# The seven-product output stage of a two-layer feed-forward kernel: order of the low parts, and which engine does sums and copies

## The chip, the cores and the metric

The kernel runs on one core of a Trainium2 chip. A core has TensorE (PE, matrix products; its weight loads are listed as PEld), VectorE (DVE), ScalarE (ACT), GpSimd (POOL) and SyncE (SP, which issues the DMAs). Each engine works through its own queue in the order in which the kernel wrote the instructions; an instruction waits for the semaphores of what it reads, and all that stands behind it on that engine waits too. The metric is the device time of one execution in microseconds (us).

## The reference

Causal attention with a decay (4 batches, 8 heads, 576 tokens, 64 wide) gives 2304 token rows of 512. Two feed-forward layers follow, each 512 to 2048 to 512:

```
x = x @ w_in;  g = h * clip(h + 3, 0, 6) / 6;  x = g @ w_out          (layer 1)
h = x @ w_in2; g = max(h, 0) + alpha * min(h, 0);  out = g @ w_out2   (layer 2)
```

All is float32. A float32 matrix product is done as three products of parts: each operand is split into a high part (rounded by ACT, `nc.scalar.copy` into a float32r tile) and a low part (operand minus high part), and high x high, high x low and low x high are added.

## The kernel before

**Tiling.** Token rows are taken in three blocks of 768 (`p` = 0, 1, 2), the 2048 hidden features in eight groups of 256 (`g`). One pair is a set `(ff, g, p)`; layer 2 ends with the eight sets of block `p` = 2, in the order `g` = 6, 7, 0, 1, 2, 3, 4, 5. A set makes the hidden values of 256 features for 768 tokens by seven block products (Strassen's scheme in the form of Winograd, 2 x 2 blocks of features and model width against two halves of tokens); each is `product`, six matmuls of 128x384. While PE does the products of one set, it does between them the output pieces of the set before, so each group of matmuls has work of another kind around it.

**The seven sets.** For the first seven of the last eight sets (`seven`), the output product too is done in seven block products (`piece7`). The hidden values are blocks of features x tokens: `gt["f", n, i]`, token half `n`, feature tile `i`. In the code's names a11 = (0,0), a12 = (0,1), a21 = (1,0), a22 = (1,1). Out of these come four sums on GpSimd (`sums`, L762): 5 = a22 + a21, 6 = (5) - a11, 7 = a11 - a21, 3 = a12 - (6). The seven operands 4 (a22), 5, 1 (a11), 6, 7, 2 (a12), 3 each get a high part by ACT (`high7`, L757) and a low part by GpSimd (`low7`, L760). The weights have four sums of their own, made early and stored in DRAM; for each set they are fetched, and split in two halves `h` by `weights7` (high L952 on ACT, low L955 on VectorE). The four plain blocks of the hidden values end with the slope, the second half of the activation (L740 on VectorE), after a first half on ACT (L731).

**Order of the work.** The kernel writes it out by hand. `now` counts steps; each character of a sequence is a step, a digit a product, `q` the next piece of the set before. In this stage the sequence is `SEQ7 = "1q5qq6qq3qq7qq2q4q"` with the pieces `PLAN7 = 4, 5, 45, 1, 6, 16, 7, 7-, 2, 3, 23`. A piece of one number is that block product for two row tiles of the half (six matmuls of 128x256), one of two numbers the third row tile of two block products, `7-` that of one. `later(d, fn)` puts instructions d steps on, in the order in which they were registered for that step; `aside` puts them behind these. So the low part of operand 6, for instance, is written seven steps after product 2 and that of 2 three steps after product 4, and GpSimd's queue in a set is: 5, low of 4, low of 5, 6, 7, low of 1, 3, low of 2, low of 6, low of 7, low of 3. In a piece's three matmuls for one tile the low part of the hidden values is read by the third.

**Where the products are summed.** A piece ends in a PSUM tile `o` (three buffers in turn: a piece can't start until the one three before it has been read out). For the first of the seven sets `flush` copies it to its place in SBUF (`kept`), for the others VectorE adds it (L922). After the seventh set, while the last set `(1, 5, 2)` runs, the seven kept products are summed into the four output blocks (`sum7`, L930): 6 = 1 + 6, 7 = 6 + 7, 6 = 6 + 5, 4 = 7 - 4, 5 = 7 + 5, 2 = 1 + 2, 3 = 6 + 3, each as one instruction of 128x512 and one of 128x256. The last set then has six plain pieces (`piece`, L842, six matmuls of 128x512), first three of token half 1, then three of half 0; each is added by VectorE to a summed block (L860) and stored.

Of the kernel before, what the change touches and what calls it, by code (L numbers as in the profile page):

```python
# [8 lines left out]
F32 = mybir.dt.float32  # L9
# [5 lines left out]
ALU = mybir.AluOpType  # L15
# [6 lines left out]
def decay_attention_ffn2_kernel(ctx, tc, qk, v, f, wi1, wo1, wi2, wo2, alpha, out):  # L22
    nc = tc.nc
# [685 lines left out]
    def later(d, fn):  # L709
        at.setdefault(now[0] + d, []).append(fn)  # L710

    def aside(d, fn):
        behind.setdefault(now[0] + int(d), []).append(fn)

    def activate(s, gt, i, n, h, d):
        ff, g, p = s
        if n not in gt and s not in seven:
            gt[n] = {}
        hold = {}

        def first():
            if s in seven:
                t = P["tp"].tile([128, NB], F32, tag="t", name="t") if (n, i) != (0, 1) else temp("wa")[:, 0:NB]
                gt["f", n, i] = t
            else:
                t = P["tp"].tile([128, NB], F32, tag="t", name="t")
            if ff == 0:
                nc.scalar.activation(out=t, in_=h(), func=AF.Relu, bias=three, scale=1.0)
                hold["g"] = t
                return  # L730
            nc.scalar.activation(out=t, in_=h(), func=AF.Relu, scale=-1.0)  # L731
            hold["g"] = t

        def second():
            g32 = hold["g"]
            if ff == 0:
                nc.vector.scalar_tensor_tensor(out=g32, in0=g32, scalar=6.0, in1=h(), op0=ALU.min, op1=ALU.mult)  # L737
            else:
                m = g * FT + i
                nc.vector.scalar_tensor_tensor(out=g32, in0=g32, scalar=alpha_sb[:, m:m + 1], in1=h(),  # L740
                                               op0=ALU.mult, op1=ALU.add)

        def third():
            gt[n][i] = P["gp"].tile([128, 2, NB], F32R, tag=f"g{n}", name=f"g{n}", bufs=3 - n)
            nc.scalar.copy(out=gt[n][i][:, 0], in_=hold["g"])  # L745
            nc.gpsimd.tensor_sub(out=gt[n][i][:, 1], in0=hold["g"], in1=gt[n][i][:, 0].bitcast(F32))  # L746

        def high7(k, t):
            if k in (2, 3):
                j = gorder[ff][1].index(g)  # L750
                o = XS[0][0].rearrange("p a b c -> p (a b c)").rearrange("p (k n) -> p k n", k=7)[:, 2 * (j % 2) + k - 2]
                o = o.rearrange("p (a n) -> p a n", a=2)
            else:
                tag = "g1" if k in (4, 5) else "g0"
                o = P["gp"].tile([128, 2, NB], F32R, tag=tag, name=tag, bufs=2 if k in (4, 5) else 3)
            gt[k] = o
            nc.scalar.copy(out=o[:, 0], in_=t)  # L757

        def low7(k, t):
            nc.gpsimd.tensor_sub(out=gt[k][:, 1], in0=t, in1=gt[k][:, 0].bitcast(F32))  # L760

        def sums():  # L762
            a11, a12, a21, a22 = (gt.get(("f", x, y)) for x in range(2) for y in range(2))
            if (n, i) == (1, 1):
                gt["f", 5] = temp("wc")[:, 0:NB]
                nc.gpsimd.tensor_add(out=gt["f", 5], in0=a22, in1=a21)
            elif (n, i) == (0, 0):
                gt["f", 6], gt["f", 7] = temp("wd")[:, 0:NB], a21
                nc.gpsimd.tensor_sub(out=gt["f", 6], in0=gt["f", 5], in1=a11)
                nc.gpsimd.tensor_sub(out=a21, in0=a11, in1=a21)  # L770
            else:
                gt["f", 3] = temp("wc")[:, 0:NB]
                nc.gpsimd.tensor_sub(out=gt["f", 3], in0=a12, in1=gt["f", 6])

        later(d, first)
        later(d + 1, second)
        if s in seven:
            k = {(1, 1): 4, (0, 0): 1, (0, 1): 2}.get((n, i))
            if k:
                more = {4: (5,), 1: (6, 7), 2: (3,)}[k]  # L780
                gap = len(more)
                later(d + 2, lambda: high7(k, hold["g"]))
                later(d + 2, sums)
                later(d + 3, lambda: low7(k, hold["g"]))
                for x in more:
                    later(d + 3 + gap, lambda x=x: high7(x, gt["f", x]))
                    later(d + 4 + gap, lambda x=x: low7(x, gt["f", x]))
            return
        later(d + 1, third)

# [77 lines left out]
    def temp(tag):  # L868
        return wtmp.tile([128, KH, 256], F32, tag=tag, name=tag).rearrange("p k n -> p (k n)")
# [16 lines left out]
    def tees(j):  # L886
        t = XS[0][1].rearrange("p a b c -> p (a b c)")[:, 4 * DM * (j % 2):4 * DM * (j % 2) + 4 * DM]
        return t.rearrange("p (a k n) -> p a k n", a=2, k=4)

    def piece7(s, gt, text):  # L890
        ff, g, p = s
        j = gorder[ff][1].index(g)
        wo, tw, kept, hd = wt[ff, g, 1], tees(j), keep7(), DM // 2
        plain = {1: (0, 0), 2: (1, 0), 3: (1, 1)}
        o = P["ps_o"].tile([128, 512], F32, tag="o", name="o")
        work = [(int(text[0]), c) for c in range(2)] if len(text) == 1 else [(int(k), 2) for k in text if k != "-"]
        for slot, (k, c) in enumerate(work):
            a = gt[k]
            if k in plain:
                t, x = plain[k]  # L900
                b = [wo[:, e, t, hd * x:hd * x + hd] for e in range(2)]
            else:
                b = [tw[:, e, WT7[k]] for e in range(2)]
            cs = slice(c * 128, c * 128 + 128)
            for e, (x, y) in enumerate(((a[:, 0], b[0]), (a[:, 0], b[1]), (a[:, 1], b[0]))):
                nc.tensor.matmul(out=o[:, hd * slot:hd * slot + hd], lhsT=x[:, cs], rhs=y,  # L906
                                 start=slot == 0 and e == 0, stop=e == 2, skip_group_check=slot > 0)
        src = o.rearrange("p (a n) -> p a n", a=2)
        if len(text) == 1:
            dst = kept[int(text)][0]  # L910
        elif text[1] != "-":
            dst = kept[text]
        else:
            dst, src = kept[int(text[0])][1], o[:, 0:hd]

        def flush():
            if j == 0 and len(text) == 1:
                nc.scalar.copy(out=dst, in_=src)
            elif j == 0:
                nc.vector.tensor_copy(out=dst, in_=src)  # L920
            else:
                nc.vector.tensor_add(out=dst, in0=src, in1=dst)  # L922

        later(0, flush)
        if s != seven[-1]:
            return

        def sum7(wait, engine, d, x, y, op):
            for part in range(2):
                later(wait, lambda part=part: engine.tensor_tensor(out=kept[d][part], in0=kept[x][part],  # L930
                                                                   in1=kept[y][part], op=op))

        if text == "16":
            sum7(1, nc.gpsimd, 6, 1, 6, ALU.add)
        if text == "7-":
            sum7(1, nc.gpsimd, 7, 6, 7, ALU.add)
            sum7(3, nc.gpsimd, 6, 6, 5, ALU.add)
            sum7(4, nc.vector, 4, 7, 4, ALU.subtract)
            sum7(5, nc.vector, 5, 7, 5, ALU.add)
        if text == "23":  # L940
            sum7(2, nc.vector, 2, 1, 2, ALU.add)
            sum7(3, nc.vector, 3, 6, 3, ALU.add)

    def weights7(s):
        ff, g, p = s
        tw = tees(gorder[ff][1].index(g))

        def fetch7():
            nc.sync.dma_start(out=tw[:, 1].bitcast(F32), in_=wt_d[g])

        def high7(h):
            nc.scalar.copy(out=tw[:, 0, 2 * h:2 * h + 2], in_=tw[:, 1, 2 * h:2 * h + 2].bitcast(F32))  # L952

        def low7(h):
            nc.vector.tensor_sub(out=tw[:, 1, 2 * h:2 * h + 2], in0=tw[:, 1, 2 * h:2 * h + 2].bitcast(F32),  # L955
                                 in1=tw[:, 0, 2 * h:2 * h + 2].bitcast(F32))

        if s == seven[0]:
            ops = conv_ops(1, 0, tags="cdabc")
            for t, names in ((0, "p2 p3"), (4, "v1 v3"), (5, "v2 u0"), (6, "v4 u1")):  # L960
                for name in names.split():
                    aside(t, ops[name])
        fetch7()
        for h in range(2):
            aside(8 + 2 * h, lambda h=h: high7(h))
            aside(9 + 2 * h, lambda h=h: low7(h))
# [156 lines left out]
```

## Time and profile before

| | us |
|---|---|
| median of 3 runs (lowest, highest) | 967.99 (966.4, 969.34) |
| the profiled execution, its own time | 969.33 |
| its span, first to last instruction | 967.5 |
| busy: PE, PEld, DVE, POOL, ACT | 948.3, 866.5, 733.1, 665.4, 550.3 |

The span is what lies between the first and the last instruction of the profiled execution; the rest of that execution's own time, 1.83 us, lies around it. Busy times are over the whole span. The seven sets and the last set take the stretch from 834 us of the span to its end; the rows below are times in us from the span's start.

### The profile page before, as it was taken

To read this page: it belongs to the slowest core of one execution; us is meant where nothing else is said; L and a number is where in the kernel's file an instruction comes from. 1 tells how busy PE (TensorE), PEld (TensorE's weight loads), DVE (VectorE), ACT (ScalarE), POOL (GpSimd) and SP (SyncE) were. 2 spreads that over 40 slices of the span, in tenths; PEclk is the share of its full clock that TensorE was granted. 3 is DMA by queue.
4 is the path that set the end of the run, shared out by engine and by line. 5 is a ranking of instruction groups with operands and counts; after the bars stand their busy time and mean duration, and the time that the engine had idled before them with its cause. 6 is when DMAs were issued, how large, how long until landed. Compare 5 with 4: busy or idle time off the path is not lost.

```text
span 967.5 us, 16523 instructions
## 1 busy us (share of the span) xinstructions
PE 948.3 (98%) x5714; PEld 866.5 (90%) x5714; DVE 733.1 (76%) x1291; ACT 550.3 (57%) x1352; POOL 665.4 (69%) x661
## 2 busy tenths in 40 slices
PE   8999999999999999999999999999999999999997
PEld 5777777789999999999999999898989999899995
DVE  7899999767787887777788573378778877576866
ACT  5888888856655555554654456545545455454441
POOL 7678998656666556684773497667675779457574
PEclk9999999999999999999999999999999999999998
DMA  6766777202354244111778540415553411646431
GB/s 212 228 202 187 227 240 226 85 23 71 137 186 185 90 172 178 63 45 42 290 255 325 205 166 34 176 62 188 196 207 103 177 37 65 251 165 260 169 159 66
DMA packets 39512, 153.71 MB, mean 159 GB/s; under 512 B 5228, under 2 KB 5228, under 8 KB 36324
## 3 DMA queue, kind: packets, MB, share of 16 engines
q1 hardware_dynamic: 39424, 152.65, 44.9%
q8 instruction: 45, 0.74, 0.3%
q14 instruction: 39, 0.32, 0.1%
q10 hardware_dynamic: 4, 0.00, 0.0%
HBM read 101.40 MB, written 47.09 MB: 153 GB/s over the span
## 4 chain that ended last, share of the span: by engine, by line
PE 83%; DVE 7%; POOL 5%; issue 3%; ACT 2%; DMA 1%; DVEq 0%; POOLq 0%; ACTq 0%; SPq 0%
PE o L840 19%; PE hA L802 18%; PE o L842 15%; PE hC L802 9%; PE hB L802 4%; PE pv L492 4%; PE tp L434 4%; PE sc L403 2%; PE sc L404 2%; PE o L906 2%; POOL g L760 1%; PE sc L415 1%; PE sc L417 1%; PE sc L405 1%; PE tr L472 1%
## 5 line engine op out<-in xcount | busy, mean ns | idle before, releaser
L746 POOL TENSOR_TENSOR g<-t,g 128x384 fp32r<-128x384 f32 x164 | 177.5, 1083 | 173.9 <-ACT g L745 167.2
L840 PE MATMUL o<-g,wo 128*128 128x384 f32 x1152 | 230.9, 339 | 1.2 <-POOL g L746 1.1
L802 PE MATMUL hA<-xh,wi 128*128 128x384 f32 x768 | 225.2, 337 | 0.6 <-ACT p L386 0.3
L840 PEld LDWEIGHTS o<-g,wo 128*128 128x128 f32 x1152 | 204.1, 188 | 2.4 <-POOL g L746 2.0
L745 ACT CAST g<-t 128x384 fp32r<-128x384 f32 x164 | 84.3, 514 | 149.4 <-DVE t L737 74.7
L842 PE MATMUL o<-wo,g 128*128 128x512 f32 x612 | 160.7, 399 | 3.4 <-DVE r L922 3.4
L802 PEld LDWEIGHTS hA<-xh,wi 128*128 128x128 f32 x768 | 141.6, 188 | 3.3 <-DVE hD L816 0.6
L842 PEld LDWEIGHTS o<-wo,g 128*128 128x128 f32 x612 | 115.6, 191 | 22.7 <-DVE r L922 3.8
L802 PE MATMUL hA<-xl,wi 128*128 128x384 f32 x384 | 129.5, 337 | 0.0
L849 DVE SCALAR_TENSOR_TENSOR r<-o,r 128x384 f32<-128x384 f32 x168 | 92.1, 551 | 47.2 <-PE o L840 46.3
L802 PE MATMUL hC<-xh,wi 128*128 128x384 f32 x384 | 114.1, 338 | 0.0
L860 DVE TENSOR_TENSOR r<-o,r 128x512 f32<-128x512 f32 x90 | 61.7, 686 | 43.2 <-PE o L842 42.9
L386 ACT ACTIVATE p<-sc,nm 128x128 f32<-128x128 f32 (+2 forms) x144 | 80.1, 561 | 19.4 <-DVE nm L379 16.4
L379 DVE TENSOR_REDUCE nm<-sc 128x1 f32<-128x128 f32 (+2 forms) x144 | 71.2, 506 | 11.7 <-PE sc L405 6.4
L802 PEld LDWEIGHTS hA<-xl,wi 128*128 128x128 f32 x384 | 72.2, 188 | 2.2
L802 PEld LDWEIGHTS hC<-xh,wi 128*128 128x128 f32 x384 | 70.9, 188 | 1.5 <-issue 0.2
L264 POOL TENSOR_TENSOR xl<-r,xh 128x384 fp32r<-128x384 f32 x59 | 68.5, 1173 | 2.1 <-ACT xh L259 1.6
L434 PE MATMUL tp<-ident,p 128*128 128x128 f32 x384 | 66.8, 277 | 0.3 <-ACT pt L449 0.3
L802 PE MATMUL hC<-xl,wi 128*128 128x384 f32 x192 | 64.8, 337 | 0.0
L807 ACT COPY s<-hA 128x384 f32<-128x384 f32 x96 | 45.8, 477 | 25.9 <-PE hA L802 25.6
L802 PE MATMUL hB<-xh,wi 128*128 128x384 f32 x192 | 57.1, 338 | 0.0
L816 DVE TENSOR_TENSOR hC<-hC,s 128x384 f32<-128x384 f32 x48 | 27.0, 563 | 37.1 <-PE hC L802 31.5
(203 smaller groups left out, 2073.3 us busy)
## 6 DMA issues: line engine op xcount, KB each, us to landing
wid<-wi SPq DMA_DIRECT2D x24, 896.0 KB
wi<-wid SPq DMA_DIRECT2D x12, 1792.0 KB
rqk<-in_qk SPq DMA_DIRECT2D x32, 608.0 KB
raw<-in_wi SPq DMA_DIRECT2D x32, 512.0 KB
raw<-in_wo SPq DMA_DIRECT2D x32, 512.0 KB
wod<-wo SPq DMA_DIRECT2D x24, 512.0 KB
wo<-wod SPq DMA_DIRECT2D x12, 1024.0 KB
vt<-in_v SPq DMA_DIRECT2D x16, 320.0 KB
```

Of the source, the lines that this page charges most:

```text
L264: e.tensor_sub(out=XS[k][1][:, b, c], in0=x, in1=XS[k][0][:, b, c].bitcast(F32))
L379: last = waits("V", nc.vector.tensor_reduce(out=nm, in_=src, axis=AX.X if n == 1 else AX.XY, op=ALU.max, negate=True), last)
L386: last = waits("A", nc.scalar.activation(out=o, in_=src, func=AF.Exp, bias=nm, scale=1.0, accum_out=dst), last)
L434: nc.tensor.transpose(tp[:, j, :], pt[:, 128 * j:128 * j + 128], ident)
L745: nc.scalar.copy(out=gt[n][i][:, 0], in_=hold["g"])
L746: nc.gpsimd.tensor_sub(out=gt[n][i][:, 1], in0=hold["g"], in1=gt[n][i][:, 0].bitcast(F32))
L802: nc.tensor.matmul(out=h, lhsT=a, rhs=b[:, x, kc], start=new and kc + e == 0, stop=kc == KH - 1 and e == 2, skip_group_check=not new)
L807: nc.scalar.copy(out=c[k], in_=h)
L840: nc.tensor.matmul(out=o[:, 0:NB], lhsT=a[:, cs], rhs=b, start=st, stop=sp)
L842: nc.tensor.matmul(out=o, lhsT=b[:, cs], rhs=a, start=st, stop=sp)
L849: later(0, lambda: nc.vector.scalar_tensor_tensor(out=acc, in0=o[:, 0:NB], scalar=1.0 / 6.0, in1=acc, op0=ALU.mult, op1=ALU.add))
L860: nc.vector.tensor_add(out=acc, in0=o, in1=acc)
```

## The change

Five edits, all in the stage of the seven sets:

- operand 6 is made by VectorE instead of GpSimd;
- the high and low parts of 6 are written two steps earlier, those of 7 one step earlier; 5 and 3 stay. GpSimd's queue in a set becomes: 5, low of 4, low of 5, 7, low of 1, 3, low of 6, low of 2, low of 7, low of 3;
- the first set's copies out of PSUM: pieces 4 and 5 go from ACT to VectorE, 16 and 23 from VectorE to ACT;
- of the last sums, 4 and 5 are written one step after piece 23 (they were at the two steps ahead of and with it), so behind the last set's slopes and behind the read-out of 23, and 2 goes from VectorE to GpSimd;
- the low parts of the weight sums go from VectorE to GpSimd.

```diff
             elif (n, i) == (0, 0):
                 gt["f", 6], gt["f", 7] = temp("wd")[:, 0:NB], a21
-                nc.gpsimd.tensor_sub(out=gt["f", 6], in0=gt["f", 5], in1=a11)
+                nc.vector.tensor_sub(out=gt["f", 6], in0=gt["f", 5], in1=a11)
                 nc.gpsimd.tensor_sub(out=a21, in0=a11, in1=a21)
...
             if k:
-                more = {4: (5,), 1: (6, 7), 2: (3,)}[k]
-                gap = len(more)
                 later(d + 2, lambda: high7(k, hold["g"]))
                 later(d + 2, sums)
                 later(d + 3, lambda: low7(k, hold["g"]))
-                for x in more:
-                    later(d + 3 + gap, lambda x=x: high7(x, gt["f", x]))
-                    later(d + 4 + gap, lambda x=x: low7(x, gt["f", x]))
+                for x, e in {4: ((5, 4),), 1: ((6, 3), (7, 4)), 2: ((3, 4),)}[k]:
+                    later(d + e, lambda x=x: high7(x, gt["f", x]))
+                    later(d + e + 1, lambda x=x: low7(x, gt["f", x]))
...
-            if j == 0 and len(text) == 1:
+            if j == 0 and text in "16723":
                 nc.scalar.copy(out=dst, in_=src)
...
             sum7(3, nc.gpsimd, 6, 6, 5, ALU.add)
-            sum7(4, nc.vector, 4, 7, 4, ALU.subtract)
-            sum7(5, nc.vector, 5, 7, 5, ALU.add)
         if text == "23":
-            sum7(2, nc.vector, 2, 1, 2, ALU.add)
+            sum7(1, nc.vector, 4, 7, 4, ALU.subtract)
+            sum7(1, nc.vector, 5, 7, 5, ALU.add)
+            sum7(2, nc.gpsimd, 2, 1, 2, ALU.add)
             sum7(3, nc.vector, 3, 6, 3, ALU.add)
...
         def low7(h):
-            nc.vector.tensor_sub(out=tw[:, 1, 2 * h:2 * h + 2], in0=tw[:, 1, 2 * h:2 * h + 2].bitcast(F32),
+            nc.gpsimd.tensor_sub(out=tw[:, 1, 2 * h:2 * h + 2], in0=tw[:, 1, 2 * h:2 * h + 2].bitcast(F32),
                                  in1=tw[:, 0, 2 * h:2 * h + 2].bitcast(F32))
```

## Rows read from the trace of the kernel before

**Rows 1.** Page, part 4: the chain that ended last, by engine.
```profile
PE 83%; DVE 7%; POOL 5%; issue 3%; ACT 2%; DMA 1%; DVEq 0%; POOLq 0%; ACTq 0%; SPq 0%
```
**Rows 2.** Waits, 834 to 967.5: who waited for whom: total us, times, longest.
```profile
POOL wc L766 <- DVE t L740: 36.3, 6, 10.7
...
PE o L906 <- POOL g L760: 6.3, 8, 1.4
...
PE o L842 <- DVE r L922: 3.4, 1, 3.4
```
**Rows 3.** Windows, one set: length, busy of PE, PEld, DVE, ACT, POOL, clock, DMA.
```profile
867.50:883.40 15.90, 15.08 (x107) 14.87 (x106) 11.84 (x21) 7.30 (x16) 10.79 (x11) 1.00 0.56 199
```
**Rows 4.** Timeline of PE: start, us, line, tiles, [idle before]; first set, third set.
```profile
841.60 1.45 PE L906 MATMUL o<-xl,g 128*128 128x256 f32 x10 [1.44 <-POOL g L760]
...
876.81 0.74 PE L906 MATMUL o<-xl,g 128*128 128x256 f32 x4 [0.82 <-POOL g L760]
```
**Rows 5.** Timeline of POOL, one set: 6, low of 2, low of 6, next 5.
```profile
870.88 1.01 POOL L769 TENSOR_TENSOR wd<-wc,t 128x384 f32<-128x384 f32 x1
...
874.78 1.02 POOL L760 TENSOR_TENSOR xh<-wa,xh 128x384 fp32r<-128x384 f32 x1
875.76 1.00 POOL L760 TENSOR_TENSOR g<-wd,g 128x384 fp32r<-128x384 f32 x1
...
883.83 1.01 POOL L766 TENSOR_TENSOR wc<-t 128x384 f32<-128x384 f32 x1 [5.12 <-DVE t L740]
```
**Rows 6.** Timeline of DVE in that set: the slope of block a12.
```profile
870.26 0.61 DVE L740 SCALAR_TENSOR_TENSOR wa<-wa,alpha_sb,hA 128x384 f32<-128x384 f32 x1 [0.18 <-ACT wa L731]
```
**Rows 7.** Timeline of POOL in the first set: operand 6.
```profile
838.61 1.02 POOL L769 TENSOR_TENSOR wd<-wc,t 128x384 f32<-128x384 f32 x1 [1.20 <-issue]
```
**Rows 8.** Lines L264, L955, L930: count, ns lowest/median/highest, first and last start.
```profile
L264 DVE TENSOR_TENSOR xl<-r,xh x25: 541/728/1640, 212.8 to 819.4; 128x384 fp32r<-128x384 f32 x25
...
L955 DVE TENSOR_TENSOR xl<-xl x14: 678/681/1375, 834.1 to 929.9; 128x512 fp32r<-128x512 f32 x14
...
L930 POOL TENSOR_TENSOR raw<-raw x2: 1287/1294/1300, 945.8 to 948.7; 128x512 f32<-128x512 f32 x2
```
**Rows 9.** Timeline of DVE at the end: sums 4 and 5, slopes, flush of 23.
```profile
950.03 2.63 DVE L930 TENSOR_TENSOR r<-raw,r 128x512 f32<-128x512 f32 x2 [1.76 <-POOL raw L930]
...
951.16 1.50 DVE L930 TENSOR_TENSOR r<-raw,r 128x256 f32<-128x256 f32 x1
952.58 0.60 DVE L740 SCALAR_TENSOR_TENSOR t<-t,alpha_sb,hB 128x384 f32<-128x384 f32 x1
...
953.71 0.41 DVE L930 TENSOR_TENSOR r<-raw,r 128x256 f32<-128x256 f32 x1
954.20 0.61 DVE L740 SCALAR_TENSOR_TENSOR t<-t,alpha_sb,hA 128x384 f32<-128x384 f32 x1
954.74 0.68 DVE L922 TENSOR_TENSOR r<-o,r 128x512 f32<-128x512 f32 x1
```
**Rows 10.** Timeline of POOL at the end: 6 = 6 + 5, first part.
```profile
950.64 1.73 POOL L930 TENSOR_TENSOR raw<-raw,r 128x512 f32<-128x512 f32 x1
```
**Rows 11.** Timeline of PE at the end: the last six pieces.
```profile
949.16 2.94 PE L842 MATMUL o<-wo,g 128*128 128x512 f32 x12
955.47 8.46 PE L842 MATMUL o<-wo,g 128*128 128x512 f32 x24 [3.38 <-DVE r L922]
```
**Rows 12.** Windows at the end; the last but two figures: the granted clock, as share.
```profile
954.00:955.00 1.00, 0.00 (x0) 0.00 (x0) 0.92 (x3) 0.32 (x2) 0.98 (x1) 0.70 0.00 0
...
961.00:962.00 1.00, 1.00 (x5) 0.77 (x5) 0.69 (x1) 0.00 (x0) 0.00 (x0) 0.89 0.03 8
```
**Rows 13.** Timeline of DVE: the last instruction on it.
```profile
963.97 0.69 DVE L860 TENSOR_TENSOR r<-o,r 128x512 f32<-128x512 f32 x1 [0.71 <-PE o L842]
```

## The prediction

> **What bounds the kernel now.** The chain of waits comes first [rows 1]: PE has 83% of it, so the end moves only where PE is idle or slowed. The list of waits over the last stretch, which all five edits touch, shows what PE waits for there [rows 2]: the low parts made by POOL (6.3 us in eight waits, all ahead of output pieces) and one read-out of a PSUM buffer by DVE (3.4 us). The windows show that one set lasts 15.90 us, of which PE is busy 15.08 [rows 3]: the 0.82 missing is one wait in each set. The PE timeline shows it: in the third set PE stands at 875.99 with piece 6 begun and goes on at 876.81, when POOL has ended the low part of 6 (875.76 + 1.00) [rows 4, 5]. The first set has a larger one: PE waits 1.44 us for the low part of 5, until 841.60 [rows 4]. POOL isn't short of time: it is busy 10.79 of 15.90 and idle 5.12 in one piece before operand 5 of the next set [rows 3, 5]. It does the right work in the wrong order.
>
> The second loss is at the end. PE stops 3.38 us before the fourth-to-last piece, because the buffer it needs holds piece 23, whose read-out (954.74, 0.68) stands in DVE's queue behind sum 4, a slope, sum 5 and the other slope [rows 9, 11]. The idle PE also loses its clock: 0.70 on the mean over 954 to 955 (so 1.0 down to 0.5 at about 954.4), back at about 961.2 [rows 12]. These are the two levels 2.4 and 1.2 GHz. Twelve matmuls took 2.94 us before the stop, 24 took 8.46 after it where twice 2.94 is 5.88 [rows 11], so the half clock costs about 2.6 us.
>
> **Order of the low parts and the sum on VectorE.** The instructions per set stay the same in number; POOL loses operand 6 (1.01) and the low part of 6 moves ahead of that of 2. POOL's queue from 870.88 on, where it had operand 6, is now 7, low of 1, 3, low of 6, at 0.97 from start to start (874.78 to 875.76 is 0.98): low of 6 runs 873.8 to 874.8, and PE asks for it at 875.99 [rows 4, 5]. That is 1.2 us of slack where 0.8 was missing. What is late next? Low of 2 then ends by 875.8 and low of 7 by 876.8, both for pieces that come after piece 6, so nothing is.
>
> Operand 6 on DVE has no row. The nearest is a subtraction of the same size with both inputs in SBUF: 0.54 alone, 0.73 at the median, 1.64 at most [rows 8]. It goes in ahead of the slope of a12, which is queued behind it and had started at 870.26 after 0.18 idle [rows 6]: 6 from 870.1 to 870.6 or 871.7, the slope then done between 871.2 and 872.3. Who waits for these: 3 on POOL, which isn't up before 872.8, and ACT's high part of 6, which low of 6 needs at 873.8. Both ends of the range cost nothing; I take 0.73 to 1.0. DVE's read-outs behind it shift by as much, within its idle time (11.84 busy of 15.90 [rows 3]).
>
> **Weight lows on POOL.** Two per set leave DVE (0.68 each, up to 1.38) and come to POOL at about 1.29 each, the price of a 128x512 subtraction there [rows 8]. They are written behind POOL's chain of the set, into the 5.12 idle before the next operand 5: 2.6 of 5.1, so they are covered. If that cover were gone they would delay operand 5 and eat the 1.2 of slack first. On DVE the two slots ahead of the slope that releases operand 5 become free, so POOL's chain starts up to 0.7 earlier: the slack grows.
>
> In the first set it is tighter. Low of 5 ended at 841.6; POOL had waited 1.20 there before operand 6 [rows 7]. Without that gap (-1.20), without 6 (-0.97), with the slope some 0.6 earlier, and with a weight low now between operand 5 and low of 4 (+1.29), it ends at about 840.1, and PE needs it at 841.60 - 1.44 = 840.16 [rows 4]. No wait, or a few tenths. The first set's copies swap between ACT and DVE, both with idle time around them: nothing.
>
> Sum of this stage: 6.3 [rows 2] less 0.4 left in the first set: **5.9 us**. Bounds: 3.5, if half of the waits of sets two to seven come back through POOL instructions slowed beside DVE, to 6.3.
>
> **The end.** DVE is idle for 1.76 until 950.03 [rows 9], so free at 948.3; before, sum 4 stood in front and waited for POOL. Now the first slope runs 948.3 to 948.9, the second starts 1.0 after its end as in the rows (953.18 to 954.20, ACT's work for it lies between), so 949.9 to 950.5, and piece 23 is read out by 951.2 instead of 955.4. PE needs this at 952.1: the 3.38 wait goes, and the third piece ends at 953.5.
>
> But the next piece needs the buffer of the first one, and its read-out is now queued behind sums 4 and 5 on DVE. Each is a 512 and a 256 instruction. Alone they cost 0.68 + 0.41 [rows 8, 9]; beside POOL's sums the pair took 2.63, in it a 256 that took 1.50 [rows 9]. So the read-out starts between 951.2 + 2.2 = 953.4 and 951.2 + 5.3 = 956.5. POOL has 6 + 5, two low parts and sum 2 in its queue without a gap from 950.64 on, so the row beside POOL is the nearest: I take 956.0, read out at 956.7. PE stops from 953.5 to 956.7, 3.2 us, nearly as long as before, one piece later.
>
> A rule of the Trainium skill bears on this choice ("SBUF — State Buffer", section "SBUF: two separate sides"): VectorE instructions with two SBUF inputs and GpSimd instructions that read SBUF share a port pair, and whoever starts first holds it for the whole instruction while the other is blocked. The 1.50 instruction agrees: it ended 0.29 after POOL's (950.64 + 1.73 = 952.37) [rows 9, 10]. By that rule the four parts of sums 4 and 5 each wait out one POOL instruction and the read-out starts at about 956.1; with no such lock, at 953.4.
>
> A stop of 3.2 us looks like the one that lost the clock, so I expect the fall again: 18 matmuls at 0.245 are 4.4, plus about 2.7 for the half clock, so PE ends at 963.8 against 963.9. Without the fall it ends at 961.1. With sums at their lowest price it ends near 958.6; at their highest, with all 18 at half clock, near 966. I take a gain of **0.2 us**, bounds -2.0 and 5.3. Sum 2 on POOL ends by 958.5, before its block is read. After the last add (963.97 [rows 13]) nothing changes.
>
> **Sum.** 5.9 + 0.2 = 6.1 off the profiled execution's 969.33 (967.5 of span, 1.83 around it): 963.2. That execution stood 1.34 above the median of the runs; off 967.99 it gives **961.9**.
>
> **Rivals.** (a) The stage as above, and the clock doesn't fall at the end, since PE stops later or a little shorter: 2.7 more, **959.2**. For it: 2.4 us of idle decided in the row, and I have 3.2 only by the upper price of the sums. Against it: that price is what the rows beside POOL show. (b) Half of the waits stay, from the first set, slower POOL instructions or a late high part of 6: **964.5**. Against it: slack of 1.2. (c) The change doesn't do what it says: the wait moves from piece 6 to 7 or 5 and keeps its size, and the end is as forecast: **967.8**, no change. Against it: low of 7 comes earlier too. (d) Slower: operand 6 on DVE and POOL's chain stretch each other. Place: POOL's seven instructions from operand 5 to low of 6. Price: POOL's 1.29 became 1.73 beside DVE [rows 8, 10], 0.44 each; seven are 3.1, less the slack of 1.2 leaves 1.9 of wait where 0.82 was, 1.1 more in each of seven sets: **975**. It decides from 2.0 us of stretch in a set on. Against it: only one DVE instruction in the stage, operand 6, has both inputs in SBUF, since the others there read PSUM; it can stretch one or two of the seven.
>
> **How the numbers follow.** Forecast 0.47, (a) 0.30, (b) 0.11, (c) 0.07, (d) 0.05. A measurement of this kernel can tell about 0.3% (2.9 us) from no change. Forecast, (a) and nearly all of (b) are faster by more: 0.87; same 0.09; slower 0.04. The likeliest case has 960.3 to 964 for itself; the range takes in (a) and most of (b): 958.3 to 964.9.
>
> **What would show it.** Right: no wait of PE for L760 in pieces 6 of the sets, 15.1 us from set to set; POOL's idle before operand 5 down to about 2.5 to 3; operand 6 on DVE under 1.7; at the end no stop before the third plain piece but one of 2 to 3.5 before the fourth, with sums 4 and 5 stretched beside POOL, and the clock at 0.5 for some 6 us. Wrong: sets still at 15.9; a PE wait for L760 in another piece; or no stop at all in the last six pieces.

## The result, and the profile after

The changed kernel takes 959.26 us (median of 6 runs, 958.74 to 960.6) against 968.25 (6 runs, 966.4 to 969.34): 9.0 us less, a ratio of 0.9913 (95% interval 0.9899 to 0.9927). The forecast was 6.1 less, 961.9. The profiled execution took 960.44, with a span of 958.7 where it was 967.5.

To see where the 8.8 us of span went, cut both traces at two places on PE: the first matmul of the first output piece of the seven sets (837.88 before, 837.99 after) and the first of the last six pieces (949.16, 941.49).

| stretch | before | after | difference |
|---|---|---|---|
| up to the first piece of the seven sets | 837.88 | 837.99 | +0.11 |
| the seven sets | 111.28 | 103.50 | -7.78 |
| last six pieces to the end | 18.34 | 17.21 | -1.13 |

The chain of waits after the change (the page's part 4) has more of PE in it than before [rows 1]: 90% where it had 83%.

```profile
PE 90%; DVE 5%; POOL 2%; issue 1%; ACT 1%; DMA 1%; DVEq 0%; ACTq 0%; POOLq 0%; SPq 0%
```

The waits of the changed kernel from 834 to its end (engine and line, what it waited for: total us, times, longest). Beside [rows 2]: PE's waits for L760, the low parts, fell from 6.3 to 0.2, POOL's wait for the slope that releases operand 5 from 36.3 to 9.7, and the stop for a read-out is still 3.2, now for L858, the read-out of a plain piece.

```profile
POOL wc L766 <- DVE t L740: 9.7, 7, 2.0
...
PE o L840 <- DVE r L858: 3.2, 1, 3.2
...
PEld o L904 <- POOL g L760: 0.4, 1, 0.4
...
PE o L904 <- POOL g L760: 0.2, 1, 0.2
```

A stretch of 15.10 in the windows (length; busy PE, PEld, DVE, ACT, POOL): PE is busy throughout, POOL for 12.96 of 15.10 where it had 10.79 of 15.90 [rows 3]. The stretch is a little more than one set: from the third set on, a set now takes 14.85 from its start to the next one's, where it took 15.91.

```profile
865.10:880.20 15.10, 15.10 (x110) 15.10 (x109) 12.02 (x21) 7.56 (x17) 12.96 (x13) 1.00 0.58 225
```

The same set on POOL: low of 5, 7, low of 6, low of 2, the second weight low, and operand 5 of the next set. Low of 6 is done at 872.06 and piece 6 begins at 873.21. The idle time before operand 5 is 1.45, with 0.69 more before the weight low (together 2.1 where 5.12 stood [rows 5]).

```profile
866.82 1.01 POOL L760 TENSOR_TENSOR g<-wc,g 128x384 fp32r<-128x384 f32 x1
867.79 1.33 POOL L770 TENSOR_TENSOR t<-t 128x384 f32<-128x384 f32 x1
...
871.03 1.03 POOL L760 TENSOR_TENSOR g<-wd,g 128x384 fp32r<-128x384 f32 x1
872.02 1.01 POOL L760 TENSOR_TENSOR xh<-wa,xh 128x384 fp32r<-128x384 f32 x1
...
876.92 1.30 POOL L953 TENSOR_TENSOR xl<-xl 128x512 fp32r<-128x512 f32 x1 [0.69 <-ACT xl L950]
879.66 1.02 POOL L766 TENSOR_TENSOR wc<-t 128x384 f32<-128x384 f32 x1 [1.45 <-DVE t L740]
```

On DVE, operand 6 and the slope queued behind it [rows 6]. Operand 6 takes 1.15 here; over all seven sets its line has 558 ns at least and 1153 at the median. POOL's instruction beside it, which makes operand 7, took 1.33 where one of that size takes 1.01.

```profile
867.09 1.15 DVE L769 TENSOR_TENSOR wd<-wc,t 128x384 f32<-128x384 f32 x1
868.17 0.60 DVE L740 SCALAR_TENSOR_TENSOR wa<-wa,alpha_sb,hA 128x384 f32<-128x384 f32 x1
```

On PE, the one wait for a low part that is left, in the first set (1.44 before [rows 4]), and the last six pieces [rows 11]: three without a stop, then 3.15, then three at 6.00 instead of 4.34.

```profile
840.49 1.45 PE L904 MATMUL o<-xl,g 128*128 128x256 f32 x10 [0.23 <-POOL g L760]
...
941.49 4.34 PE L840 MATMUL o<-wo,g 128*128 128x512 f32 x18
948.99 6.00 PE L840 MATMUL o<-wo,g 128*128 128x512 f32 x18 [3.15 <-DVE r L858]
```

On DVE at the end: the read-out of piece 23 (954.74 before [rows 9]), the four parts of sums 4 and 5 in 4.85, the read-outs queued behind them, the last add [rows 13].

```profile
942.79 0.68 DVE L920 TENSOR_TENSOR r<-o,r 128x512 f32<-128x512 f32 x1
943.39 4.85 DVE L928 TENSOR_TENSOR r<-raw,r 128x512 f32<-128x512 f32 x4
948.16 1.27 DVE L858 TENSOR_TENSOR r<-o,r 128x512 f32<-128x512 f32 x2
...
955.08 0.69 DVE L858 TENSOR_TENSOR r<-o,r 128x512 f32<-128x512 f32 x1 [0.77 <-PE o L840]
```

The granted clock in windows (last but two figures) [rows 12]: full until 949.0, 3.2 us after PE stopped, half until about 952.4. Before, it fell 2.3 us after the stop and stayed down for 6.8.

```profile
948.00:949.00 1.00, 0.01 (x1) 0.04 (x1) 1.00 (x3) 0.00 (x0) 1.00 (x1) 1.00 0.00 0
949.00:950.00 1.00, 1.00 (x3) 0.81 (x4) 1.00 (x2) 0.00 (x0) 1.00 (x2) 0.51 0.28 109
...
952.00:953.00 1.00, 1.00 (x5) 0.75 (x4) 0.64 (x1) 0.00 (x0) 0.00 (x0) 0.78 0.60 231
```

### The profile page after: what moved, and what is told of

The parts are those of the page before. It is cut to its first block, busy times and chain, and to the rows that moved or that the text cites. A ratio compares the mean times of both kernels' runs of the same rounds, so it can differ in the third digit from the quotient of the medians.

```text
span 958.7 us, 16492 instructions
## 1 busy us (share of the span) xinstructions
PE 946.3 (99%) x5714; PEld 865.6 (90%) x5714; DVE 732.3 (76%) x1282; ACT 551.8 (58%) x1352; POOL 681.1 (71%) x670
## 4 chain that ended last, share of the span: by engine, by line
PE 90%; DVE 5%; POOL 2%; issue 1%; ACT 1%; DMA 1%; DVEq 0%; ACTq 0%; POOLq 0%; SPq 0%
PE hA L800 20%; PE o L838 20%; PE o L840 14%; PE hC L800 10%; PE o L904 5%; PE hB L800 5%; PE tp L434 4%; PE pv L492 4%; PE sc L403 2%; PE sc L404 2%; PE sc L415 1%; PE sc L417 1%; PE sc L405 1%; PE tr L472 1%; POOL xl L264 1%
## 5 line engine op out<-in xcount | busy, mean ns | idle before, releaser
L858 DVE TENSOR_TENSOR r<-o,r 128x512 f32<-128x512 f32 x90 | 61.7, 686 | 42.6 <-PE o L840 41.9
L264 POOL TENSOR_TENSOR xl<-r,xh 128x384 fp32r<-128x384 f32 x59 | 68.6, 1175 | 2.1 <-ACT xh L259 1.5
```

What stands on the lines that cost most here:

```text
L264: e.tensor_sub(out=XS[k][1][:, b, c], in0=x, in1=XS[k][0][:, b, c].bitcast(F32))
L858: nc.vector.tensor_add(out=acc, in0=o, in1=acc)
```

## The experiments

For each kernel "sets" is the length of the seven sets on PE and "end" what follows to the end of the span, cut as above, in its profiled execution. The medians of the experiments are of 4 runs each, taken on three chips. The kernel before had 968.75 beside the order alone, the old order, the old end and the busy PE; 968.37 beside the weight lows on VectorE; 968.24 beside the other four.

A median holds more than the two stretches. In the eleven profiled executions the first piece of the seven sets starts between 836.4 and 838.9, although no edit changes an instruction before 834. So differences of medians below about 1 us decide nothing here by themselves; "sets" and "end" do.

| kernel | median | sets | end |
|---|---|---|---|
| before | 968.25 | 111.28 | 18.34 |
| changed | 959.26 | 103.50 | 17.21 |
| order alone, on the kernel before | 962.17 | 105.31 | 17.29 |
| changed, old order | 960.91 | 104.19 | 16.98 |
| changed, old order, operand 6 on GpSimd | 963.55 | 107.39 | 18.26 |
| changed, weight lows on VectorE | 960.55 | 104.18 | 17.09 |
| changed, old end | 960.78 | 103.52 | 17.34 |
| changed, PE kept busy in the stop | 958.4 | 103.51 | 15.64 |
| changed, other PSUM banks | 958.53 | 103.50 | 15.00 |
| changed, early sums | 956.66 | 103.50 | 14.30 |
| changed, early sums and other banks | 955.61 | 103.53 | 13.22 |

**The order alone**, on the kernel before:

```diff
-                more = {4: (5,), 1: (6, 7), 2: (3,)}[k]
-                gap = len(more)
...
-                for x in more:
-                    later(d + 3 + gap, lambda x=x: high7(x, gt["f", x]))
-                    later(d + 4 + gap, lambda x=x: low7(x, gt["f", x]))
+                for x, e in {4: ((5, 4),), 1: ((6, 3), (7, 4)), 2: ((3, 4),)}[k]:
+                    later(d + e, lambda x=x: high7(x, gt["f", x]))
+                    later(d + e + 1, lambda x=x: low7(x, gt["f", x]))
```

> The kernel before with nothing but the new order of the low parts (operand 6 still on GpSimd, weight lows and the end as before). Theory A, the order is what counts: low of 6 takes the place of low of 2 in GpSimd's queue and ends about 1.0 us earlier, at 875.8 where TensorE asks at 875.8 to 876.0, so the wait at piece 6 falls from 0.82 to 0.1 or less in each set; the wait of 1.44 for low of 5 in the first set stays, and the stop of 3.4 at the end stays. Set to set 14.9 us; time about 962 (6 less than before). Theory B, the moves to VectorE and GpSimd are needed as well: half of each wait stays, 965 or more.

962.17 (ratio 0.9931, 0.9913 to 0.9949), sets 105.31. PE has one wait for a low part left, that of the first set, and the stop at the end:

```profile
841.32 1.46 PE L904 MATMUL o<-xl,g 128*128 128x256 f32 x10 [1.45 <-POOL g L760]
...
949.23 7.41 PE L840 MATMUL o<-wo,g 128*128 128x512 f32 x24 [3.38 <-DVE r L920]
```

So the order is sufficient to end the matmuls' waits at piece 6 in all sets, theory A as written. A set takes 14.95 from start to start (14.9 was said), 0.1 more than in the changed kernel: the weight loads still stand some 0.07 at piece 6. The order alone gives 6.0 of the 7.8 us.

**Everything but the order:**

```diff
+                more = {4: (5,), 1: (6, 7), 2: (3,)}[k]
+                gap = len(more)
...
-                for x, e in {4: ((5, 4),), 1: ((6, 3), (7, 4)), 2: ((3, 4),)}[k]:
-                    later(d + e, lambda x=x: high7(x, gt["f", x]))
-                    later(d + e + 1, lambda x=x: low7(x, gt["f", x]))
+                for x in more:
+                    later(d + 3 + gap, lambda x=x: high7(x, gt["f", x]))
+                    later(d + 4 + gap, lambda x=x: low7(x, gt["f", x]))
```

> The changed kernel with the old order of the low parts (operand 6 on VectorE, weight lows on GpSimd, new end). Theory A in its strict form (only the order counts): the wait at piece 6 comes back, 1.06 us in each of seven sets, time about 959.3 + 7 = 966. Theory C (two sufficient causes): operand 6 has left GpSimd's queue and the chain starts about 0.7 earlier, since the weight low is out of VectorE's way, so low of 6 is in time even behind low of 2: no wait, time 959.3 within 0.6.

Sets 104.19. The matmuls wait twice for a low part, both times in the first set: 0.23 for that of 5, as in the changed kernel, and 0.42 at piece 6.

```profile
PE o L906 <- POOL g L760: 0.7, 2, 0.4
```

So the waits at piece 6 don't come back from the second set on, and the strict form of theory A falls. The order is sufficient and not necessary: the two moves do the same for the sets by themselves, and the order brings only 0.7 us on top of them. The median of 960.91 is 1.65 above the changed kernel and outside theory C's 959.3 within 0.6. The sets account for 0.7 of that, and the profiled end, 0.2 shorter, for nothing. The rest stays open; none of its four runs had a mean granted clock of 1.000, as two of six of the changed kernel's had.

**The old order, and operand 6 on GpSimd**, so beside the edit above:

```diff
-                nc.vector.tensor_sub(out=gt["f", 6], in0=gt["f", 5], in1=a11)
+                nc.gpsimd.tensor_sub(out=gt["f", 6], in0=gt["f", 5], in1=a11)
```

> The changed kernel with the old order of the low parts and operand 6 back on GpSimd; weight lows on GpSimd and the new end stay. It tells apart why the old order did no harm with operand 6 on VectorE. If it is that operand 6 has left GpSimd's queue (0.97 per set): TensorE waits 0.5 to 0.8 again at piece 6 in each set, time about 965. If the earlier start of GpSimd's chain is enough (0.7 earlier, the weight low being out of the way of VectorE's slope): waits of 0.1 to 0.3 in the sets, about 1 in the first set, time 961 to 962.5.

963.55, between the two forecasts, and the profile is between them too: sets 107.39, half of the 7.8 us. Operand 6 off GpSimd's queue and the earlier start of its chain both count: without either the sets take 111.28, with the earlier start alone 107.39, with both 104.19. The waits of this kernel from 834 on show something else (total us, times, longest): PE's weight loads waited 3.9 us for low parts, eight times, its matmuls only 1.7, three times.

```profile
PEld o L906 <- POOL g L760: 3.9, 8, 1.1
...
PE o L906 <- POOL g L760: 1.7, 3, 0.9
```

The sets are 3.89 longer than those of the changed kernel. The loads' row says 3.9 - 0.4 = 3.5, the matmuls' row 1.7 - 0.2 = 1.5. The loads tell nearly all of the loss, the matmuls do not: in the last five sets they stood only 0.12 to 0.13 each, too short for this list, and yet a set took 15.24 instead of 14.85.

**Weight lows on VectorE:**

```diff
-            nc.gpsimd.tensor_sub(out=tw[:, 1, 2 * h:2 * h + 2], in0=tw[:, 1, 2 * h:2 * h + 2].bitcast(F32),
+            nc.vector.tensor_sub(out=tw[:, 1, 2 * h:2 * h + 2], in0=tw[:, 1, 2 * h:2 * h + 2].bitcast(F32),
```

> The changed kernel with the low parts of the weight sums back on VectorE; order, operand 6 on VectorE and the new end stay. It tells which edit removed the first set's wait of 1.44 for the low part of 5. If the weight lows must leave VectorE (they stand ahead of the slopes there): the wait in the first set stays at 0.8 or more, the sets from the second on have none, time 960 to 960.5. If operand 6 leaving GpSimd's queue is enough: 0.5 or less, time 959.3 to 959.6.

960.55, sets 104.18, all of the 0.7 in the first set: there PE waits 0.85 again (first row, PE), since a weight low of 1.38 stands on DVE ahead of the slopes (second row, DVE). The first forecast holds (0.8 or more, 960 to 960.5).

```profile
839.56 1.46 PE L904 MATMUL o<-xl,g 128*128 128x256 f32 x10 [0.85 <-POOL g L760]
```

```profile
835.13 1.38 DVE L953 TENSOR_TENSOR xl<-xl 128x512 fp32r<-128x512 f32 x1
```

**The old end:**

```diff
+            sum7(4, nc.vector, 4, 7, 4, ALU.subtract)
+            sum7(5, nc.vector, 5, 7, 5, ALU.add)
         if text == "23":
-            sum7(1, nc.vector, 4, 7, 4, ALU.subtract)
-            sum7(1, nc.vector, 5, 7, 5, ALU.add)
-            sum7(2, nc.gpsimd, 2, 1, 2, ALU.add)
+            sum7(2, nc.vector, 2, 1, 2, ALU.add)
```

> The changed kernel with the last sums as they were before (4 and 5 ahead of the slopes, 2 on VectorE). By the traces the new end is worth 1.3 us, all of it from a later and shorter fall of the clock: time 960.6, PE stop of 3.4 before the third plain piece, clock at 0.5 for 5 to 7 us. Rival: the end is worth nothing in the median, because the fall differs from run to run by as much: 959.3, and the sets alone explain the whole 9 us.

960.78, close to the 960.6 of the first forecast, and the stop stands before the third plain piece again (3.37). Yet its profiled end, 17.34, is only 0.13 longer than the 17.21 of the changed kernel, and its clock was at half for 3.4 us, not 5 to 7. How long the clock stays at half differs between executions with the same end. The old end takes 17.29 and 17.34 where that was 3.4 us (the order alone, and this kernel) and 18.34 where it was 6.8 (the kernel before). The new end takes 16.98 to 17.21 with 3.4 us (old order, weight lows, changed) and 18.26 with 6.8 (old order with operand 6 on GpSimd). So for the same fall of the clock the new end is worth 0.1 to 0.4 us. Nearly all of the 1.13 that the end gained between the first two profiles is the shorter fall.

The new end may make a short fall likelier. With the old end the mean granted clock of an execution was 0.996 in 19 of 29 runs, 0.998 in 10 and never higher; with the new end it was 0.996 in 5 of 18, 0.998 in 10 and 1.000 in 3. That would fit the 1.5 us between the medians, but it isn't shown: the runs are few, and a low clock elsewhere in the execution counts in that mean too (see other PSUM banks below).

**PE kept busy in the stop**, by 14 matmuls of zeros into a bank that nobody reads:

```diff
-    early = {}
+    early, still0 = {}, []
...
             nc.vector.memset(still, 0.0)
+            still0.append(still)
...
+        if s == sets[-1] and (n, c) == (1, 2):
+            t0 = P["ps_h"].tile([128, 512], F32, tag="C", name="busy", bufs=1)
+            for _ in range(14):
+                nc.tensor.matmul(out=t0.rearrange("p (a b) -> p a b", a=4), lhsT=still0[0],
+                                 rhs=still0[0].unsqueeze(1).broadcast_to([128, 4, 128]), start=True, stop=True)
```

> The changed kernel with 14 idle matmuls (zeros, 128x512, into a free PSUM bank that nobody reads) behind the third plain piece, so that TensorE isn't idle in the stop of 3.15 us. If the low clock is what the last pieces lose: clock at 1.0 to the end, the last 18 matmuls in 4.4 instead of 6.0, time 958.7 in every run (about 1.6 below a run with the fall, 0.5 below the median), and less spread between runs. Rival, the matmuls after the stop are slow for another reason, or the added matmuls delay the next piece: no gain, or up to 1 us slower.

958.4 (three runs at 958.3 to 958.5, one at 959.4); 958.7 in every run was said. The last three pieces start as late as ever, 7.50 us after the first of the six, and take 4.42 instead of 6.00:

```profile
945.25 3.19 PE L845 MATMUL busy<-still 128*128 128x512 bf16 x14
948.56 4.42 PE L841 MATMUL o<-wo,g 128*128 128x512 f32 x18
```

So the half clock alone cost the profiled execution 1.58 us. Part of the spread goes with it: of the changed kernel's runs, the two with a mean granted clock of 1.000 took 958.74 and 958.8, the four with 0.996 to 0.998 took 959.2 to 960.6. It isn't all of the spread: with the clock at 0.999 to 1.000 the four runs of this kernel still differ by 1.1.

**Other PSUM banks** for the last three pieces:

```diff
-        o = P["ps_o"].tile([128, 512], F32, tag="o", name="o")
+        spare = {0: ("ps_h", "C"), 1: ("ps_d", "D"), 2: ("ps_h", "B")}[c] if s == sets[-1] and n == 0 else None
+        if spare:
+            o = P[spare[0]].tile([128, 512], F32, tag=spare[1], name="o", bufs=1)
+        else:
+            o = P["ps_o"].tile([128, 512], F32, tag="o", name="o")
```

> The changed kernel with the last three pieces in three other PSUM banks (of the hidden products, free by then), so that they don't wait for read-outs. If the read-out behind sums 4 and 5 is what stops TensorE: the stop of 3.15 us goes and one of some 2 us stays, for the low part of the last slope that GpSimd makes behind the sum 6 + 5; the clock stays up; the end is then set by VectorE's queue of sums and adds: time 957.5 to 958.3 (1 to 2 below the changed kernel). Rival, VectorE's queue sets the end in any case and the stop is only its mirror: within 0.5 of 959.3.

958.53, 0.2 above the forecast's upper end and 0.3 below the rival's range. The stop of 3.15 is gone, and what stays on PE are two short waits for the last low parts (first two rows, PE) instead of one of some 2 us; the clock keeps up there. The end is 2.2 shorter than in the changed kernel, but with PE kept busy it was already 1.57 shorter with the stop in place. So the stop itself is worth only some 0.6: the sums on DVE still take 4.88 (third row), the read-outs wait behind them, and DVE's last add ends 2.0 after PE. The rival is right on that, and the forecast on what stops PE. The median shows less of the 2.2; in this profiled execution the clock was at half from 11.0 to 14.4 as well, far ahead of the stage, and the first piece started at 838.9. A mean granted clock below 1 therefore need not come from the end.

```profile
947.54 0.97 PE L844 MATMUL o<-wo,g 128*128 128x512 f32 x3 [0.33 <-POOL g L746]
948.95 3.29 PE L844 MATMUL o<-wo,g 128*128 128x512 f32 x13 [0.45 <-POOL g L746]
```

```profile
944.30 4.88 DVE L932 TENSOR_TENSOR r<-raw,r 128x512 f32<-128x512 f32 x4
```

**Early sums:**

```diff
-            sum7(3, nc.gpsimd, 6, 6, 5, ALU.add)
+        if text == "45":
+            sum7(1, nc.gpsimd, 3, 3, 5, ALU.add)
+        if text == "16":
+            sum7(1, nc.vector, 2, 1, 2, ALU.add)
         if text == "23":
...
-            sum7(2, nc.gpsimd, 2, 1, 2, ALU.add)
```

> The changed kernel with fewer sums at the end: 3 + 5 on GpSimd and 2 + 1 on VectorE are done while the last set runs, so that after piece 23 there are 4 = 7 - 4, 5 = 7 + 5 and 3 = 3 + 6 alone and GpSimd's two last low parts come 2 us earlier. The buffers are as before, so the read-out still stands behind sums 4 and 5. By the port between VectorE and GpSimd (VectorE's sums stretched only as long as GpSimd runs beside them): the four parts take 2.5 to 3.5 instead of 4.85, the stop falls from 3.15 to 1 to 2 and the clock mostly stays up: time 957 to 958. If the stretch has another cause: 4.85 and 3.15 stay, time 959.

956.66, 0.3 below what was forecast by the port between the two engines; the four parts, the stop and the clock are as that forecast said, and its rival (4.85 and 3.15 stay) is out. GpSimd has only two low parts (2.48 together) beside DVE's sums, and their four parts take 2.78 instead of 4.85 (DVE); the stop is 1.73 and the clock stays at 1.0 (PE):

```profile
943.09 2.78 DVE L928 TENSOR_TENSOR r<-raw,r 128x512 f32<-128x512 f32 x4
```

```profile
946.62 4.42 PE L840 MATMUL o<-wo,g 128*128 128x512 f32 x18 [1.73 <-DVE r L858]
```

**Both together:**

> Early sums and other PSUM banks together: no stop in the last six pieces, TensorE done some 8.7 us after the first plain piece (13.5 in the changed kernel), VectorE's last add 1 to 2 us after it. Time 955 to 956, below both kernels. If VectorE's queue sets the end all the same: 957.

955.61 (ratio to the kernel before 0.9872, 0.9858 to 0.9887): below both kernels, and as forecast. The last six pieces run as one block, and DVE's four last adds end 1.3 us behind it:

```profile
940.68 8.77 PE L844 MATMUL o<-wo,g 128*128 128x512 f32 x36
```

```profile
948.30 2.47 DVE L862 TENSOR_TENSOR r<-o,r 128x512 f32<-128x512 f32 x4
```

## Why the prediction was right, and where it was off

The direction, the places and the mechanism came as written; the size was 9.0 where 6.1 was said. Of the 2.7 by which the span's gain is larger than forecast, 1.9 belong to the sets and 0.9 to the end; the stretch ahead of them gave 0.1 back. The time is that of rival (a), but in the profiled execution not for (a)'s reason, since the clock did fall at the end. Only the two of six runs with a mean granted clock of 1.000 can be (a).

**The sets, mis-sized: 7.8 measured, 5.9 said.** The step that failed is "Sum of this stage: 6.3 less 0.4". The 6.3 is the idle time of the matmuls, counted from the end of the matmul before. Matmuls overlap: a piece of six takes 0.71 from its start to the next start (873.21 to 873.92 in the changed kernel), 0.118 each, while one lasts 0.28. So when a matmul is late, the first 0.16 of the delay hides behind the one before it. And behind a wait the next matmul starts 0.22 after the late one instead of 0.118, so that four last 0.74 [rows 4] where they would last 0.63: another 0.11. From the start of piece 6 to that of the next product it is 1.80 before (875.59 to 877.39) and 0.71 after: 1.09 lost, where the idle time said 0.82. The weight loads show nearly all of it. They overlap less (0.188 each, four in 0.53), so only some 0.07 of a wait hides there: in the kernel before

```profile
876.81 0.53 PEld L906 LDWEIGHTS o<-xl,g 128*128 128x128 f32 x4 [1.03 <-POOL g L760]
```

and over the sets (engine and line, what was waited for: total us, times, longest)

```profile
PEld o L906 <- POOL g L760: 7.9, 8, 1.6
```

7.9 less the 0.4 that stays is 7.5, and 7.78 was gained. The kernel with half of the waits left shows the same (3.5 against 3.89). That row stood in the view that gave the 6.3. The sign "15.1 us from set to set" was mis-sized in the same way: it became 14.85.

**What is late next: nothing, right.** Low of 6 ended 1.15 before piece 6 began, and no other piece waits. The kernel without the new order shows that the prediction was even too careful to name the order as the remedy: the moves that it costed at nothing remove the same waits.

**Operand 6 on VectorE: inside the bounds (0.54 to 1.64), above the value taken (0.73 to 1.0).** It took 1.15 at the median and 0.56 once, when GpSimd was idle for 0.23 beside it. That agrees with the rule of the Trainium skill that the prediction weighed ("SBUF — State Buffer", section "SBUF: two separate sides"): operand 6 waits out the GpSimd instruction that is running (in the set shown, the low part of 5: it ends at 867.83 and operand 6 at 868.24), and GpSimd's next one is stretched in turn (1.33 for 1.01). It cost nothing, as said.

**Weight lows and the first set: right.** GpSimd's idle time covers them (2.1 of it is left, where 2.5 to 3 was said), and 0.23 of wait stayed in the first set.

**The end: stop right, clock off by 1.1 us.** The read-out was to start at 956.0 and the stop to last 3.2. PE had come 7.67 earlier by then, and the read-out started at 948.16 + 7.67 = 955.83; the stop was 3.15. Sums 4 and 5 took 4.85 of the 2.2 to 5.3. The clock fell as said, but later and for less: at half for 3.4 us instead of some 6, so 1.6 lost instead of 2.7. That it was less here is luck as far as the prediction goes: executions with the same end had it at half for 3.4 or for 6.8 us, and their ends differ by about 1.1. For equal falls the new end gains 0.1 to 0.4, which takes in the 0.2 that was said. Nor is the 2.4 us of idle that rival (a) took from the row a fixed time: the clock fell between 2.2 and 4.3 us after the stop began. So this term can't be had to better than about 1 us from one profile.

**Rivals.** (b) and (c) didn't occur; (d)'s stretch is real (operand 6 and one GpSimd instruction per set), and at 0.3 us far from the 2.0 from which it would have decided.

## What to carry to other kernels

Take a stall of TensorE from its weight loads or from start to start, not from the idle time of its matmuls: with overlapping matmuls, each stall here counted short by 0.27 us, and of a short one (0.39 lost) only 0.12 was to be seen on the matmuls, below what the list of waits shows. Before a wait is put down to one cause, look for a second edit that removes it too: here two sufficient ones were made at once, and 7.1 of the 7.8 us would have come without the one that names the change. At the tail, move sums off the path rather than between engines that hinder each other: doing them while there was still matmul work gave 2.6 us more (2.9 of the end), and free PSUM banks another 1.0. And compare two tails only at the same fall of the clock.

## What the hardware showed that was not expected

In seven profiled executions (the kernels before and changed, and the five variants with one of their two ends and no other edit there) TensorE stopped once for 3.15 to 3.38 us in the last six pieces. The granted clock fell 2.2 to 4.3 us after the stop began, three times only when work had resumed, and stayed at half for 3.4 us in five of them and for 6.8 in two. A stop of 1.73 us left it at 1.0 in the profiled execution, and 14 matmuls of zeros in a stop kept it up.

These 14 matmuls, of no use to the result, made the kernel faster than the changed one by 0.9 us in the median. VectorE's four parts of two sums took 4.85 us beside GpSimd's back-to-back work and 2.78 with only two GpSimd instructions beside them, with the same operands.
